# Loads issued earlier, two scale computations and one product shifted, in a fused attention and SwiGLU kernel

## The chip, the core and the metric

The kernel runs on one core of one Trainium2 chip. The metric is the device time of one execution in microseconds; the kernel before has a median of 1759.77 us over 3 runs (1759.59 to 1762.96). The core's engines are PE (matrix products), DVE, ACT and POOL (elementwise work on vectors), and SP, which here only issues DMAs. Each engine executes its own instructions in the order in which they are written; semaphores tie the engines together.

## The reference

Two branches on the same input x (2048 rows of 576), mixed row by row by a gate.

```python
x = A_x                                              # (1, 2048, 576)
g = sigmoid((x * gate_w).sum(-1, keepdims=True))
a = A_ref(x, wq, wk, wv, wo, beta)                   # attention with memory
b = (silu(x @ w_gate) * (x @ w_up)) @ w_down         # 576 -> 4608 -> 576
return g * a + (1 - g) * b

def A_ref(...):              # 32 heads of 18, 4 segments of 512 rows
    for s in range(4):
        logits = qs @ ks.T * 18 ** -0.5 + causal_mask
        a_dot = softmax(logits) @ vs
        a_mem = (phi(qs) @ M) / (phi(qs) @ z + 1e-6)     # phi(t) = t + 1 if t > 0 else exp(t)
        o = sigmoid(beta) * a_mem + (1 - sigmoid(beta)) * a_dot
        M, z = M + phi(ks).T @ vs, z + phi(ks).sum(rows)
    return o @ wo
```

## The kernel before

All operands are float32. The kernel keeps the accuracy by splitting an operand into a high and a low part and summing three products (high·high, high·low, low·high). The parts of the FFN's first two products are 16 bit, and so that they stay in range, each weight and x is first multiplied by a power of two, which is found from the data. Those factors live in columns of the tile `sc`: `sx` for x, `sw[i]` for the weights of four f-tiles (i = 0 to 8), and `iw[i]` is the inverse of both.

**Segments, 0 to 232 us.** For each of the four segments of 512 rows come nine chains of products for q and k (`qk`, 14 matmuls at L172 each, ended by conversions on ACT, DVE and POOL), and eight steps for v (`v_step`, n = 0 to 7, also L172, into banks 5, 6, 7 in turn, evacuated by ACT L434, L435 and DVE L436, and in the last four by DVE L440 too). `mem_step` (L506 and DVE L509 to L513) follows each v step in segments 1 to 3. Meanwhile the factors are found: `gauge` takes sums of squares or peaks of x and of the first weights (DVE L135, ACT L132), `total` adds them up, and `power` adds over the partitions with one small matmul (L141, into bank 7) and takes a power of two on DVE (L142 to L146). In segment 1 `power(sx)` comes after v step 1 and `power(sw[0])` after v step 5. In segment 2 the last 64 rows of x's 576 are fetched for the first half (`rest_load`), summed on POOL (`rest_sum`) and converted on ACT L197 and DVE L198 (`rest_split`); the table `RSTEP` says in which chain of the nine each of them is issued (a negative number is a sum).

**Half 0 of the FFN, 232 to about 906 us; half 1, about 911 to 1600 us.** The rows are worked in two halves (`HALF`), each with a loop over 36 f-tiles of 128 columns of w_gate and w_up. One f-tile is seven products of blocks, in place of eight, of sums and differences of blocks of x and of the weights (`seven`: six matmuls at L1303 of the kept part, one at L1306 of the 64 last rows), and after each comes a `tick`. A tick calls `beat`, and a beat does three things: it runs the functions that were deferred to it (`defer(k, fn)` is k beats on), issues groups of the down product (L1088, added up by DVE L1097), and moves the attention on by one or more steps when its credit is full. There are 8 beats to an f-tile. PE's order, and that of every other engine, is the order in which these calls are made.

For half 0, `w_make` splits the weights of the next f-tile (POOL L318, ACT L322, DVE L326) and stores them (L330) for half 1, where `w_fetch` reads them back (L821). The down weights of f are loaded with `d_load` (L266, into one of two slots `draw`), split by `d_split` (ACT L1069, DVE L1070) and stored (L1071); half 1 loads them back with L1076. `glance` loads weights of later f-tiles in full (eight loads, slots `looks`) and sums their squares on ACT (L132). Each load is issued by SP, whose queue holds also the stores, which wait there for their data.

With a position in the triple of f-tiles q = f % 3 and a tick k, the calls in half 0 are

```python
if (q, k) in ((0, 3), (1, 3), (2, 1)):
    draw[f] = d_load(f)
if (q, k) in ((1, 1), (1, 7), (2, 5)):
    g = f - 1 if k == 1 else f
    ds[half, g] = d_split(g, draw.pop(g))
```

In the last two f-tiles of half 0, `rest_second` loads the last rows of x for the second half (L1259) and converts them (ACT L1271). The first matmuls of half 1 follow the evictions L1377, L1380 (ACT) and L1384 (DVE) of the seven products.

**Attention.** `att_gen` is a generator; its step tau is one of five banks of a unit u of two heads (64 units). Most units are direct: `t_bank` computes the logits keys by queries (L957), ACT takes the exponential (L961), POOL masks (L969), DVE and POOL split it into p1 and p2 (L1055, L1057), and four steps after the unit's last bank `pv_step` multiplies all five with v (L985, L987). Ahead of that `s_bank` has found the largest logit of each row (L846 on PE, L864 on DVE). In half 1 every even unit is turned instead: its logits are exponentiated queries by keys, split (ACT L898, DVE L902, POOL L903) and transposed by DMAs (L907), and `pv_turned` multiplies (L919, L920). `v_fetch` (L254) loads v for four units at a time into one of two tiles, every 20 steps.

**End, about 1676 to 1757 us.** Attention and memory are added, multiplied with wo (L172 again), mixed with the FFN by the gate and stored (L1465).

Of the kernel before, what the change touches and what calls it, by code (L numbers as in the profile page):

```python
# [28 lines left out]
FT = 36  # L29
# [38 lines left out]
def gated_mix(ctx, tc, xT, xrest, wf, wfr, wfh, wd, wv, wo, beta, cmask, ident, bmask, out):  # L68
# [274 lines left out]
    with ExitStack() as st:  # L343
# [270 lines left out]
            rest_16(XR[j], rr[((0, 0), (0, 0), (1, 1), (0, 1), (1, 0), (1, 1), (0, 1))[j]])  # L614

        XR = [None] * 7
        RSTEP = {4: (0, 3, -1), 5: (5, -4, 1), 6: (-2, 4), 7: (2, -6), 8: (6,)}
        rb, rs = {}, {}

        def b_load(i):  # L620
# [67 lines left out]
        for s in range(NSEG):  # L688
            upd = upd_gen(s - 1) if s else None
            casts = []  # L690
            for n, (m, u) in enumerate(chains):
                mid = []
                if s == 0:
                    for z in loads.get(n, []):
                        z()
                    if n + 3 < 9:
                        mid.append(lambda n=n: q_split(*chains[n + 3]))
                    if n in halves:
                        mid.append(lambda n=n: v_split(*halves[n]))
                if s == 1 and n < 3:  # L700
                    cast = masks(*((0, 3), (3, NT), (0, 0))[n])
                    casts.append(cast)
                if s == 1 and 3 <= n < 6:
                    mid.append(casts[n - 3])
                if (s, n) == (1, 7):
                    mid.append(betas)
                mid += scan_step(17 * s + n)
                if (s, n) == (1, 7):
                    mid.append(lambda: total(sx, 0, 20))
                if s == 2:  # L710
                    if n == 4:
                        mid.append(lambda: total(sw[1], 29, 38))
                    if n == 6:
                        mid.append(lambda: power(sw[1], lone_tile([P, 1])))
                        mid.append(lambda: back(1))
                    if n == 2:
                        rest_load()
                    if n > 2 and blocks:
                        mid.append(lambda z=blocks.pop(0): b_step(*z))
                    for j in RSTEP.get(n, ()):  # L720
                        mid.append(lambda j=j: rest_split(j) if j >= 0 else rest_sum(-j))
                if s == 3:
                    if n < 4:
                        first_load(n)
                    for j, z in FSPLIT.get(n, []):
                        if j in (0, 3, 5):
                            mid.append(lambda j=j, z=z: first_split(j, z))
                    for j, z in FSUM.get(n, []):
                        mid.append(lambda j=j, z=z: first_sum(j, z))
                    for j, z in FSPLIT.get(n, []):  # L730
                        if j in (1, 2, 4):
                            mid.append(lambda j=j, z=z: first_split(j, z))
                if s < 3:
                    for kt in ((0, 1), (2, 3), (4,))[n - 6] if s == 0 and n > 5 else (n - 4,) if s and n > 3 else ():
                        raws["x", kt] = x_load(s + 1, kt)
                qk(s, m, u, mid)
                flush(2)
                scan_load(17 * s + n)
                if upd is not None and n > 0:
                    next(upd, None)  # L740
            if s == 3:
                qst_.close()
                rp = pool(ctx, "rp", 4, side="right")
                wop = pool(ctx, "wop", 8, side="right")
                kq = pool(ast, "kq", 1, side="right")
                for i in range(NST):
                    if i < 2:
                        qst.append(kq.tile([P, 2, L], BF, name=f"qst{i}"))
                    if i < 2:
                        kst.append(kq.tile([P, 2, L], BF, name=f"kst{i}"))  # L750
                for i in range(2):
                    mbs.append(kq.tile([P, 8], F32, name=f"mb{i}"))
                wraw_of[0] = [w_load(0, u) for u in range(2)]
                for z in range(2):
                    rhs.append(wop.tile([P, 7, P], F16, name=f"rh{z}", bufs=1))
                start = w_make(0)
            for n in range(8):
                hf, i = divmod(n, 4)
                flush()
                v_step(s, hf, i)  # L760
                scan_load(17 * s + 9 + n)
                if s == 1:
                    if n == 1:
                        power(sx, lone_tile([P, 1]))
                    if n == 2:
                        total(sw[0], 20, 29)
                    if n == 5:
                        power(sw[0], lone_tile([P, 1]))
                        back(0)
                if s:  # L770
                    mem_step(s, n // 2, n % 2)
                if s < 3:
                    if n == 0:
                        xs_of[s + 1] = x_tiles(s + 1)
                    if 1 <= n < 6:
                        x_split(xs_of[s + 1], n - 1, raws["x", n - 1])
                else:
                    if n == 4:
                        wraw_of[1] = [w_load(1, u) for u in range(2)]
                    if n < 2:  # L780
                        first_split(6, n)
                    elif n < 6:
                        if n < 4:
                            nc.gpsimd.memset(rhs[n - 2][96:], 0.0)
                        if n == 3:
                            r_fetch(0)
                        if n - 2 < len(kst):
                            nc.gpsimd.memset(kst[n - 2], -1.0)
                    if n > 2:
                        for z in stack_loads(0)[2 * n - 6:2 * n - 4]:  # L790
                            nc.sync.dma_start(*z)
                    for _ in range((0, 0, 2, 3, 3, 3, 3, 3)[n]):
                        if start[0][0] < 8:
                            start.pop(0)[1]()
# [5 lines left out]
    with ExitStack() as st:  # L800
# [76 lines left out]
        turned = set()  # L877
# [128 lines left out]
        def att_gen():  # L1006
            N = 10 * NB
            for tau in range(N + TL + VL + 5):
                u, n = divmod(tau, 5)
# [18 lines left out]
                if z >= 0 and z % 10 == 9:  # L1028
                    o_step(z // 10)
                z = tau - TL - VL - 1  # L1030
                if z % 5 == 4 and 0 <= z < N and z // 5 not in turned:
                    for k in range(z - 4, z + 1):
                        pv_step(k)
# [4 lines left out]
                z = tau - TL  # L1038
# [243 lines left out]
        def glance(i, k):  # L1282
            f, u = 4 * i + k // 2, k % 2
            box = []

            def load():
                box.append(x_slot(*next(looks), F32).rearrange("p a b -> p (a b)")[:, :NT * P])
                nc.sync.dma_start(box[0].rearrange("p (k n) -> p k n", n=P), wf[f][:, u])

            return [((0, 0, 1, 2, 3, 4, 4, 5)[k], load),  # L1290
                    ((2, 2, 3, 4, 5, 6, 6, 7)[k], lambda: square(box[0], 20 + 9 * i + k))]

        looks = cycle([(6, 0), (6, 1), (5, 0), (5, 1)])
# [17 lines left out]
        for pos, (half, f) in enumerate(seq):  # L1311
# [7 lines left out]
            if nxt:  # L1319
# [4 lines left out]
                if half == 0 and f + 2 < FT:  # L1324
                    wraw_of[f + 2] = [None, None]
                    for u in range(2):
                        plan.append(((2, 5)[u], lambda u=u, f=f: wraw_of[f + 2].__setitem__(u, w_load(f + 2, u))))
            i = 1 + pos // 3
            if half == 0 and pos % 3 == 0 and 2 <= i < FT // 4:
                for k in range(8):  # L1330
                    plan += glance(i, k)
            if half == 0 and pos % 3 == 1 and 2 <= i < FT // 4:
                plan += [(1, lambda i=i: total(sw[i], 20 + 9 * i, 28 + 9 * i)),
                         (5, lambda i=i: power(sw[i], ts_tile([P, 1]))), (6, lambda i=i: back(i))]
# [5 lines left out]
            if pos == 34:  # L1340
                XR2 = [None] * 7
                third = rest_second(XR2)
                plan += [(7, fn) for o, fn in third if o < 0]
            if pos == 35:
                plan += [(o, fn) for o, fn in third if o >= 0]
            for o, fn in plan:
# [3 lines left out]
            def tick():  # L1350
                k = step[0]
                step[0] += 1
                if k == 0:
                    while stores:
                        nc.sync.dma_start(*stores.pop(0))
                if half == 0:
                    if (q, k) in ((0, 3), (1, 3), (2, 1)):
                        draw[f] = d_load(f)
                    if (q, k) in ((1, 1), (1, 7), (2, 5)):
                        g = f - 1 if k == 1 else f  # L1360
                        ds[half, g] = d_split(g, draw.pop(g))
                elif (q, k) in ((1, 0), (1, 2), (2, 1)):
                    g = f - 1 if k == 0 else f
                    ds[half, g] = d_fetch(g)
                if half and k > 1:
                    opened[0] = 1
                beat(k, half)
# [157 lines left out]
```

## Time and profile before

| | |
|---|---|
| median of 3 runs | 1759.77 us |
| the profiled execution | 1760.42 us, of it span 1758.7 us |
| mean granted PE clock | 0.997 |
| PE busy | 1717.3 us, 98% |
| DVE | 1316.9 us, 75% |
| ACT | 1024.8 us, 58% |
| POOL | 843.9 us, 48% |
| DMA | 321.89 MB, mean 183 GB/s |

"Busy" adds up the instructions of an engine. In a row of the waits stand the engine and line that waited, the tile and line that ended the wait, the sum, the number of waits and the longest. In a row of the timeline stand start, duration, engine, line, operation with its tiles and shapes, number of instructions, and in brackets how long the engine had been idle before it and who ended that. SPq is SP's queue of instructions that issue DMAs; its times are those of issuing, not of the transfer.

### The profile page before, as it was taken

The page shows a single profiled execution, that of the slowest core. Times are in us where ns is not written, and L with a number is a line of the kernel's source. Part 1 is how long each engine was busy: PE and PEld are TensorE (multiplying, and loading weights), DVE is VectorE, ACT ScalarE, POOL GpSimd, SP SyncE. Part 2 cuts the span into 40 slices and gives each one's busy share as a digit, 9 for nine tenths or more (in the row PEclk, how much of TensorE's full clock was granted, in tenths as well). Part 3 has the DMA queues.
Part 4 walks back from the last instruction along what each step waited for, and adds up shares of the span by engine and source line. Part 5 has one row for each costly group of instructions (what it writes and reads, how often), then busy time and mean ns, then how long its engine had stood idle before and what let it go on. Part 6 is the DMA issues. An engine that isn't in the chain of part 4 may idle for free.

```text
span 1758.7 us, 34840 instructions
## 1 busy us (share of the span) xinstructions
PE 1717.3 (98%) x12241; PEld 1217.9 (69%) x12241; DVE 1316.9 (75%) x3239; ACT 1024.8 (58%) x1800; POOL 843.9 (48%) x1065
## 2 busy tenths in 40 slices
PE   9999999999999999999989999999999999999999
PEld 7888856656765676567657757756756766776699
DVE  6778676778878878888876877777767777775455
ACT  7757575766676666655754565555556465454411
POOL 3335551245645554665542765555546465553121
PEclk9999999999999999999999999999999999999999
DMA  8666775776676666545544487577677569654544
GB/s 286 227 219 222 233 254 192 222 229 190 180 242 219 197 186 198 183 141 156 168 149 157 121 187 167 145 196 159 142 185 196 127 162 203 168 129 129 180 137 140
DMA packets 341667, 321.89 MB, mean 183 GB/s; under 512 B 193396, under 2 KB 258676, under 8 KB 341492
## 3 DMA queue, kind: packets, MB, share of 16 engines
q1 hardware_dynamic: 341492, 319.67, 63.4%
q8 instruction: 96, 1.57, 0.4%
q14 instruction: 79, 0.65, 0.1%
HBM read 188.51 MB, written 104.86 MB: 167 GB/s over the span
## 4 chain that ended last, share of the span: by engine, by line
PE 72%; DVE 7%; ACT 6%; DMA 5%; issue 3%; SPq 3%; POOL 3%; DVEq 0%; ACTq 0%; POOLq 0%
PE bank L1303 28%; PE bank L1088 21%; PE bank L172 8%; PE bank L1306 5%; PE bank L846 3%; PE bank L957 2%; PE bank L985 1%; DMA draw<-in_wd_dram 1%; DMA xo<-in_wf_dram 1%; POOL p L1057 1%; PE bank L987 1%; SPq L1023 1%; PE bank L919 1%; ACT L1296 1%; POOL ws L318 1%
## 5 line engine op out<-in xcount | busy, mean ns | idle before, releaser
L1088 PE MATMUL bank<-dw,hh 128*128 128x320 f32 (+1 forms) x2304 | 510.5, 314 | 8.8 <-DVE ya L1097 6.8
L1088 PEld LDWEIGHTS bank<-dw,hh 128*128 128x128 f32 x2304 | 380.6, 190 | 34.2 <-DVE ya L1097 10.4
L1088 PE MATMUL bank<-dw,hl 128*128 128x320 f32 (+1 forms) x1152 | 341.0, 296 | 0.5 <-DVE hl L125 0.5
L1057 POOL TENSOR_TENSOR p<-pe,p 128x512 f16<-128x512 f32 x220 | 274.2, 1247 | 81.6 <-DVE p L1055 61.2
L961 ACT ACTIVATE pe<-bank 128x512 f32<-128x512 f32 x220 | 130.4, 593 | 218.4 <-PE bank L957 195.9
L1097 DVE TENSOR_TENSOR ya<-bank,ya 128x320 f32<-128x320 f32 x352 | 157.6, 452 | 99.6 <-PE bank L1088 97.1
L1088 PEld LDWEIGHTS bank<-dw,hl 128*128 128x128 f32 x1152 | 218.5, 190 | 1.0 <-DVE hl L125 1.0
L1306 PE MATMUL bank<-xr,rh 128*128 128x512 f16 x504 | 191.6, 380 | 0.0
L969 POOL TENSOR_SCALAR_AFFINE_SELECT pe<-pe 128x256 f32<-128x256 f32 (+1 forms) x220 | 92.2, 419 | 205.6 <-ACT pe L961 201.6
L864 DVE CUSTOM_DVE_ANT_0 junk<-bank,cm 128x128 bf16<-128x128 f32 (+2 forms) x352 | 169.7, 482 | 15.0 <-PE bank L846 9.9
L318 POOL TENSOR_TENSOR ws<-raw 128x256 f32<-128x256 f32 x72 | 66.6, 925 | 152.9 <-DMA raw<-in_wf_dram 89.6
L846 PE MATMUL bank<-kst,qst 108*128 108x512 bf16 (+3 forms) x512 | 125.2, 300 | 2.6 <-ACT pe L961 2.1
L1188 DVE TENSOR_TENSOR hl<-row,hh 128x512 fp32r<-128x512 f32 x120 | 108.5, 904 | 15.8 <-ACT hh L1187 15.4
L1055 DVE CAST p<-pe 128x512 f16<-128x512 f32 x220 | 106.3, 484 | 0.0
L1392 DVE TENSOR_TENSOR row<-bank,row 128x512 f32<-128x512 f32 x72 | 49.7, 690 | 73.6 <-ACT bank L1391 73.3
L957 PE MATMUL bank<-qst,kst 111*128 111x512 bf16 (+3 forms) x352 | 104.2, 303 | 0.0
L1387 ACT ACTIVATE row<-bank 128x512 f32<-128x512 f32 x72 | 42.9, 596 | 96.4 <-PE bank L1306 96.4
L172 PE MATMUL bank<-xo,qhi 128*128 128x512 f32 x288 | 91.8, 399 | 0.2 <-DVE xo L125 0.2
L1306 PEld LDWEIGHTS <-rh 128*128 128x128 f16 x504 | 49.4, 98 | 59.8 <-issue 0.6
L1391 ACT ACTIVATE bank<-bank 128x512 f32<-128x512 f32 x72 | 41.9, 582 | 82.2 <-PE bank L1306 80.3
L903 POOL TENSOR_TENSOR xo<-xr,xo 128x512 f16<-128x512 f32 x60 | 70.9, 1181 | 34.2 <-DVE xo L902 25.5
L416 POOL TENSOR_TENSOR q<-qr,q 128x512 bf16<-128x512 f32 x36 | 47.2, 1311 | 78.2 <-ACT q L415 64.6
(1067 smaller groups left out, 4119.2 us busy)
## 6 DMA issues: line engine op xcount, KB each, us to landing
xo<-in_wf_dram SPq DMA_DIRECT2D x65, 320.0 KB
dc<-dw SPq DMA_DIRECT2D x36, 576.0 KB
dw<-dc SPq DMA_DIRECT2D x36, 576.0 KB
raw<-in_wf_dram SPq DMA_DIRECT2D x72, 256.0 KB
rh<-rc SPq DMA_DIRECT2D x72, 168.0 KB
draw<-in_wd_dram SPq DMA_DIRECT2D x36, 288.0 KB
xo<-in_xT_dram SPq DMA_DIRECT2D x33, 256.0 KB
vd<-vps SPq DMA_DIRECT2D x8, 912.0 KB
```

The costliest lines, as they stand in the source:

```text
L172: nc.tensor.matmul(t, st[n], mv[n], start=(n == 0), stop=(n == 13))
L846: nc.tensor.matmul(t[:, c:c + w], qs[:KR, pr, P * i:P * i + P], ks[:KR, pr, 0:w], start=True, stop=True)
L864: nc.vector.tensor_tensor_reduce(junk.bitcast(BF)[:, :w], t[:, c:c + w], cm[:, L - w:L], 1.0, -3.0e38, OP.add, OP.max, m[:, k:k + 1])
L957: nc.tensor.matmul(t[:, c:c + w], ks[:KR + 3, pr, P * j:P * j + P], qs[:KR + 3, pr, P * j:L], start=True, stop=True)
L961: nc.scalar.activation(pe, t, AF.Exp, scale=SCALE)
L1055: nc.vector.tensor_copy(p1, pe)
L1057: nc.gpsimd.tensor_sub(p2, pe, p1)
L1088: nc.tensor.matmul(t, p, q[:, cs], start=(f == CH * c and n == 0), stop=(f == CH * c + CH - 1 and n == 2))
L1097: nc.vector.tensor_add(ya[:, i, cs], t, ya[:, i, cs])
L1188: defer(k + 1, lambda: nc.vector.tensor_sub(lo, src, f32(hi)))
L1303: nc.tensor.matmul(t, w[:, p, z], x[z][:, q], start=first and n == 0, stop=False, skip_group_check=True)
L1306: nc.tensor.matmul(t, rem[:, RPOS[j]], XR[j], start=False, stop=True, skip_group_check=True)
```

## The change

1. `RSTEP` and `rest_load`: in segment 2 the load of the last rows moves from chain 2 to chain 0, and the seven conversions and four sums, before in chains 4 to 8, are spread over chains 2 to 8.
2. `power(sx)` in segment 1 comes after v step 3 (before: 1), `power(sw[0])` and `back(0)` after v step 6 (before: 5).
3. In `att_gen` the products with v of a direct unit whose preceding unit is turned are issued one step later.
4. The first four of `glance`'s eight loads are issued one or two beats sooner; the first two of them in the f-tile before.
5. The first two loads of `rest_second` are issued three beats sooner.
6. The loads of the down weights are issued at (0, 1), (1, 0) and, for the next f-tile, (1, 5), where before they were at (0, 3), (1, 3) and (2, 1).

Arithmetic, tiles and the number of instructions stay the same.

```diff
-        RSTEP = {4: (0, 3, -1), 5: (5, -4, 1), 6: (-2, 4), 7: (2, -6), 8: (6,)}
+        RSTEP = {2: (0, 3), 3: (5, -1), 4: (1,), 5: (-4,), 6: (4, -2), 7: (2, -6), 8: (6,)}
...
-                    if n == 2:
+                    if n == 0:
                         rest_load()
...
                 if s == 1:
-                    if n == 1:
+                    if n == 3:
                         power(sx, lone_tile([P, 1]))
                     if n == 2:
                         total(sw[0], 20, 29)
-                    if n == 5:
+                    if n == 6:
                         power(sw[0], lone_tile([P, 1]))
                         back(0)
...
                 z = tau - TL - VL - 1
+                z -= z // 5 > 0 and (z - 1) // 5 - 1 in turned
                 if z % 5 == 4 and 0 <= z < N and z // 5 not in turned:
                     for k in range(z - 4, z + 1):
                         pv_step(k)
...
-            return [((0, 0, 1, 2, 3, 4, 4, 5)[k], load),
+            return [((-2, -1, 0, 1, 3, 4, 4, 5)[k], load),
                     ((2, 2, 3, 4, 5, 6, 6, 7)[k], lambda: square(box[0], 20 + 9 * i + k))]
...
+            if half == 0 and pos % 3 == 2 and 1 <= i < FT // 4 - 1:
+                looked = [z for k in range(8) for z in glance(i + 1, k)]
+                plan += [(7 + o, fn) for o, fn in looked if o < 0]
             if half == 0 and pos % 3 == 0 and 2 <= i < FT // 4:
-                for k in range(8):
-                    plan += glance(i, k)
+                plan += [z for z in looked if z[0] >= 0]
...
-                plan += [(7, fn) for o, fn in third if o < 0]
+                plan += [(4, fn) for o, fn in third if o < 0]
...
-                    if (q, k) in ((0, 3), (1, 3), (2, 1)):
-                        draw[f] = d_load(f)
+                    if (q, k) in ((0, 1), (1, 0), (1, 5)):
+                        g = f + (q == 1 and k == 5)
+                        draw[g] = d_load(g)
```

## The prediction

> **What bounds the kernel now.** I read the page's first part, then the waits of PE, the waits of ACT, and last the timeline around each place that the change touches.
>
> ```profile
> PE 1717.3 (98%) x12241; PEld 1217.9 (69%) x12241; DVE 1316.9 (75%) x3239; ACT 1024.8 (58%) x1800; POOL 843.9 (48%) x1065
> ```
>
> PE runs 1717.3 of the span's 1758.7 us. It executes in the order written, so the work behind an idle stretch moves up by as much as the stretch shrinks, unless another wait ends later. No edit here takes a matmul away; only PE's 41.4 us of not being busy, and stretches in which it runs slowly, can change. The waits of PE (engine, line, releaser: us in total, times, longest) say who causes them:
>
> ```profile
> PE bank L1088 <- DVE ya L1097: 6.8, 13, 1.4
> PE bank L1303 <- ACT bank L1377: 6.2, 6, 2.0
> PE bank L987 <- POOL p L1057: 5.1, 4, 2.0
> PE bank L172 <- DVE r L436: 3.9, 2, 2.6
> PE bank L1303 <- DVE bank L1384: 2.3, 2, 2.0
> ...
> PE bank L141 <- DVE dn L509: 1.2, 1, 1.2
> ...
> PE bank L172 <- DVE sc L142: 0.6, 1, 0.6
> ```
>
> The first row is not touched. The other six are each the end of a chain that one of the edits moves.
>
> **Down weights (half 0).** In six steps PE waits for ACT's eviction L1377 at the head of an f-tile. Two of those rows and the largest, with what stands ahead of it (start, duration, engine, [idle before and releaser]):
>
> ```profile
> 236.47 1.46 PE L1303 MATMUL bank<-xo,wo__2589 128*128 128x512 f16 x6 [0.80 <-ACT bank L1377]
> 248.22 1.46 PE L1303 MATMUL bank<-xo,wo__2841 128*128 128x512 f16 x6 [0.53 <-ACT bank L1377]
> ...
> 599.10 0.55 SPq L297 DMA_DIRECT2D rc<-rt  x1
> ...
> 601.34 0.46 SPq L266 DMA_DIRECT2D draw<-in_wd_dram  x1
> ...
> 607.95 0.77 ACT L1069 ACTIVATE dw<-draw,sc 128x576 fp32r<-128x576 f32 x1 [2.35 <-DMA draw<-in_wd_dram]
> 608.63 0.58 ACT L1377 ACTIVATE bank<-bank 128x512 f32<-128x512 f32 x1
> 609.26 1.46 PE L1303 MATMUL bank<-xo,wo__7517 128*128 128x512 f16 x6 [2.00 <-ACT bank L1377]
> ```
>
> ACT takes L1069 ahead of the eviction and stands 2.35 us for the weights that SP began to load at 601.34; PE pays 2.00 of it. The edit issues that load two beats earlier, ahead of the store at 599.10, so 2.2 us or more sooner; the two slots of draw are free by then, since the last reader of each (L1070) runs two beats ahead of the new place. In the waits of ACT these stalls are
>
> ```profile
> ACT xo L132 <- DMA xo<-in_wf_dram: 20.3, 15, 2.1
> ...
> ACT dw L1069 <- DMA draw<-in_wd_dram: 6.7, 5, 2.3
> ```
>
> five in all. The first two PE waits of the group (0.80 and 0.53) stand at the start of half 0, where no L1069 is late, so 6.2 − 1.33 = 4.9 us of PE's wait hang on it. What is late next is 601.34 − 599.10 = 2.24 us of advance against 2.35 us of wait, about 0.1 left in the worst place. I take −4.6; bounds −4.9 and −2.5 (half of the advance lost because the raw weight loads now queue behind).
>
> **Rests of x, second half (the step from half 0 to half 1).**
>
> ```profile
> 900.74 0.32 SPq L330 DMA_DIRECT2D wc<-wo__11429  x1
> ...
> 903.59 2.14 SPq L1259 DMA_DIRECT2D raw<-in_xr_dram  x2
> ...
> 907.90 0.72 ACT L1271 ACTIVATE xr<-raw,sc 128x512 f16<-128x512 f32 x1 [1.61 <-DMA raw<-in_xr_dram]
> ...
> 909.47 0.58 ACT L1380 ACTIVATE row<-bank 128x512 f32<-128x512 f32 x1
> ...
> 910.37 0.70 DVE L1384 TENSOR_TENSOR bank<-bank,row 128x512 f32<-128x512 f32 x1
> ...
> 911.12 2.56 PE L1303 MATMUL bank<-xo,wo__11503 128*128 128x512 f16 x6 [1.99 <-DVE bank L1384]
> ...
> 913.90 1.87 PE L1303 MATMUL bank<-xo,wo__11503 128*128 128x512 f16 x6
> ```
>
> The chain is load, L1271, L1380, L1384, PE. Three beats earlier in the list is not three beats on the chip: SP executes in order, and in the changed program the two loads stand right behind the store at 900.74, which waits for its data. So they gain 903.59 − 901.06 = 2.5 us, more than the 1.61 that ACT waits. ACT's earlier work ends at 907.90 − 1.61 = 906.29, so L1384 can end up to 1.6 earlier and PE's 1.99 shrinks to about 0.4: −1.6. Behind the wait the six matmuls take 2.56 and 1.87 where the rows above show 1.46, a stretch at half the clock: 2.56 + 1.87 − 2 × 1.46 = 1.5 us, which goes if the wait goes. Sum −3.1; bounds −3.5 and −1.0 (a transfer as late as before by 1 us).
>
> **The product with v one tick later (half 1).** PE waits for POOL's second half of p (L1057) at four odd units. The first and the last:
>
> ```profile
> 1025.09 0.19 PE L987 MATMUL bank<-v,p 128*128 128x38 bf16 x1 [0.28 <-POOL p L1057]
> ...
> 1296.48 0.19 PE L987 MATMUL bank<-v,p 128*128 128x38 bf16 x1 [2.05 <-POOL p L1057]
> ...
> 1296.90 2.64 PE L1303 MATMUL bank<-xo,wo__16820 128*128 128x512 f16 x6
> ...
> 1299.75 1.80 PE L1303 MATMUL bank<-xo,wo__16864 128*128 128x512 f16 x6
> ```
>
> The first has no turned unit ahead of it and isn't moved; the other three hold 5.1 − 0.28 = 4.8 us. One attention tick holds at least one group of seven matmuls, 1.46 plus 0.22 of PE work, and mostly two, against a longest wait of 2.05, so I count all of it gone. Behind the 2.05 again stands a half-clock stretch: 2.64 + 1.80 − 2.92 = 1.5. Together −6.3; bounds −6.5 and −4.
>
> The matmul moved last in every fourth unit also frees the tile that SP's fetch of v overwrites (L254, bufs 2), and that fetch keeps its tick. SP now stands there longer, and behind it in its queue are the transposes L907, the stack loads L1023, the operand loads L821, the down weights L1076 and L304:
>
> ```profile
> SPq L254 <- PE bank L846: 49.4, 7, 11.9
> ...
> 1041.70 0.57 SPq L821 DMA_DIRECT2D wo__13336<-wc  x1
> ...
> 1046.63 1.47 PE L1303 MATMUL bank<-xo,wo__13336 128*128 128x512 f16 x6 [0.62 <-DMA wo__13336<-wc]
> ...
> 1102.75 0.57 SPq L821 DMA_DIRECT2D wo__14252<-wc  x1
> ...
> 1108.85 1.46 PE L1303 MATMUL bank<-xo,wo__14252 128*128 128x512 f16 x6
> ```
>
> SP already stands 49.4 us there in seven places (the page names the last PE event, L846). One more tick is 1.7 to 3.4 us for each. A load that came too late needed 1046.63 − 1041.70 = 4.9 us; the tightest that I found behind a fetch, issued at 1102.75 and used at 1108.85, has 6.1, so 1.2 to spare. Most have more. Price +0.3; bounds 0 and +3.
>
> **Powers of two (segment 1).** The waits of 1.2 (L141 <- L509) and 0.6 (L172 <- L142) lie at the old places: −1.8. But the little product L141 writes bank 7, and the v products take banks 5, 6, 7 in turn; after steps 3 and 6 the bank just filled is bank 7, so each power must wait for that product's eviction. How long that takes is seen at an untouched step:
>
> ```profile
> 101.78 0.83 PE L506 MATMUL bank<-Mm,ph 128*128 128x152 f32 x6
> ...
> 102.80 0.46 DVE L436 TENSOR_TENSOR r<-bank,vps 128x288 f32<-128x288 f32 x1 [0.29 <-ACT vps L435]
> ```
>
> The product's end is the start of L506, 101.78; its last reader ends at 103.26, so 1.48 us. Step 6 has one reader more (L440), some 0.2. Two waits of 1.48 and 1.7 come, 1.8 goes: +1.4. Bounds −1.8 (nothing new waits) and +3.
>
> **Rest of x, first half (segment 2).** The load goes two chains up, and the seven rest conversions spread over chains 2 to 8.
>
> ```profile
> 140.22 2.32 DVE L198 SCALAR_TENSOR_TENSOR xr<-xo,sc,xr 32x512 f16<-32x512 f32 x2
> ...
> 157.54 0.45 DVE L436 TENSOR_TENSOR r<-bank,vps 128x288 f32<-128x288 f32 x1
> 158.04 1.86 PE L172 MATMUL bank<-vw,xo 128*128 128x288 f32 x12 [2.58 <-DVE r L436]
> ```
>
> DVE is busy without a pause from there to 157.54, and PE's 2.58 is that backlog. A step of two L198 is 2.32; half of it, 1.2, is what moving two conversions ahead of the backlog is worth, less 0.2 for a new wait ahead of it: −1.0. Bounds −2.6 (the whole wait) and 0.
>
> **Looks at the weights:** four of the eight loads go one or two beats sooner. The 20.3 us that ACT waits at L132 shrink, but none of PE's seven rows names L132 or something right behind it: 0; bounds −1.5 and +0.5.
>
> **Sum.** −4.6 − 3.1 − 6.3 + 0.3 + 1.4 − 1.0 = −13.3. The profiled execution took 1760.42 (span 1758.7 and 1.7 around it), 0.65 over the median 1759.77. So span 1745.4, profiled 1747.1, and median 1746.5.
>
> [...] Half clock follows the waits of 1.99 and 2.05, but not those of 2.00 (609.26) and 2.58 (158.04, where 12 matmuls take 1.86). So length alone doesn't decide it. [...]
>
> **The rivals.**
> 1. The slow stretches are not caused by the waits in front of them and stay, wherever they fall: 3.0 of the sum goes, 1749.5. Two of four such waits are followed by none, which speaks for it; that they begin at the wait, against. [...] Chance 0.12.
> 2. The loads take their time from other loads: each one that goes ahead holds back a raw weight or an operand. Then the down-weight gain halves (2.3), the rest's goes (3.1), the powers cost 3 instead of 1.4 and the fetches 3 instead of 0.3: −13.3 + 9.7 = −3.6, 1756.2. For it: ACT and POOL wait on loads in many places. Against: the bytes are the same, only their order changes. Chance 0.12.
> 3. Slower. The fetch of v, held a tick longer, passes its hold on to PE: eight times the hold of up to 3.4 less 1.2 to spare, 2.2, and half a clock behind each, 1.5, are 29.6: −13.6 + 29.6 = +16, 1776. It decides from 1.7 us for each fetch on. Against it are the 6.1 us at the tightest place and fetches that already stand 7 us on average with hardly a PE wait by a load. Chance 0.06.
> 4. The moved loads don't start sooner, because each still stands behind a store that waits in SP's queue: d_load and rests bring nothing, −13.3 + 7.7 = −5.6, 1754.2. The new order speaks against it at 599.10 and 900.74. Chance 0.05.
>
> **How the numbers follow.** The forecast, 1746.5, has 0.65. A measurement of this kernel tells 0.2%, 3.5 us, from no change, so faster is below 1756.3: the forecast, rivals 1 and 4, and a third of rival 2, 0.65 + 0.12 + 0.05 + 0.04 = 0.86, of which I leave 0.04 to bounds that add up badly: 0.82. Same takes most of rival 2 and some of that: 0.10; slower 0.08. The range: all low bounds together would be −4.9 − 3.5 − 6.5 − 1.8 − 2.6 − 1.5 = −20.8; they won't all come, so 1740.5. Upward to rivals 1 and 4 and the edge of 2: 1756.
>
> **What would show it.** Right: ACT's waits at L1069 (6.7) near 0; no wait of L987 on L1057 but the first; PE's wait at 911 under 0.6 and 1.46 behind it; two waits of about 1.5 at L141 on bank 7; the wait at 158 about 1 us shorter. Wrong: new PE waits on loads of wo_ in half 1 behind L254, or half-clock stretches at other places. I am wrong altogether if PE's waits shrink by 10 and the span doesn't follow.

## The result, and the profile after

The kernel after takes 1750.11 us (median of 4 runs, 1749.31 to 1750.78) against 1760.08 for the kernel before in the same measurement. The ratio is 0.994, 95% interval 0.9923 to 0.9957, so 10 us were won, inside the range and 3.6 us short of the forecast. The span of its profile is 1748.7 us against 1758.7.

The page and the waits of PE for the kernel after (from L1031 on, line numbers are one to four higher than before: L1303 is now L1304, L1377 is L1381, L1384 is L1388, L1069 is L1070, L1088 is L1089, L1057 is L1058):

```profile
PE 1714.6 (98%) x12241; PEld 1217.6 (70%) x12241; DVE 1326.4 (76%) x3239; ACT 1024.4 (59%) x1800; POOL 841.7 (48%) x1065
```

```profile
PE bank L1089 <- DVE ya L1098: 7.0, 13, 1.4
PE bank L172 <- DVE r L436: 2.2, 2, 1.1
...
PE bank L846 <- DMA kst<-stw: 2.0, 1, 2.0
PE bank L141 <- DVE r L436: 1.9, 1, 1.9
...
PE bank L141 <- DVE gl L440: 1.5, 1, 1.5
PE bank L1304 <- ACT bank L1381: 1.3, 2, 0.8
...
PE bank L1304 <- DVE bank L1388: 0.8, 2, 0.5
...
PE bank L1304 <- DMA wo__17650<-wc: 0.6, 1, 0.6
...
PE bank L987 <- POOL p L1058: 0.3, 1, 0.3
```

Four rows of before have shrunk as forecast: L1304 behind ACT from 6.2 to 1.3, L987 behind POOL from 5.1 to 0.3, L172 behind L436 from 3.9 to 2.2, and L1304 behind DVE from 2.3 to 0.8. The two rows of the powers at their old places are gone. Both waits of the powers on bank 7 are new, and they were expected. A wait of 2.0 us for a stack load kst is new and was not. One more is the prediction's own sign of being wrong, a new wait on a load of wo_ in half 1: it came once, with 0.6 us (wo__17650), while the 0.6 us of wo__13336 went. The same places in the timeline of the kernel after:

```profile
100.13 0.38 PE L141 MATMUL bank<-sc 128*128 128x1 f32 x2 [1.91 <-DVE r L436]
100.38 0.91 PE L506 MATMUL bank<-Mm,ph 128*128 128x114 f32 x6
101.08 2.70 PE L172 MATMUL bank<-vw,xo 128*128 128x290 f32 x12
...
111.51 0.35 PE L141 MATMUL bank<-sc 128*128 128x1 f32 x2 [1.52 <-DVE gl L440]
...
160.47 1.86 PE L172 MATMUL bank<-vw,xo 128*128 128x288 f32 x12 [1.11 <-DVE r L436]
...
238.67 1.46 PE L1304 MATMUL bank<-xo,wo__2589 128*128 128x512 f16 x6 [0.81 <-ACT bank L1381]
...
596.13 0.47 SPq L266 DMA_DIRECT2D draw<-in_wd_dram  x1
596.71 0.57 SPq L297 DMA_DIRECT2D rc<-rt  x1
...
603.06 0.76 ACT L1070 ACTIVATE dw<-draw,sc 128x576 fp32r<-128x576 f32 x1
603.73 0.58 ACT L1381 ACTIVATE bank<-bank 128x512 f32<-128x512 f32 x1
...
604.65 1.46 PE L1304 MATMUL bank<-xo,wo__7517 128*128 128x512 f16 x6
...
905.27 1.46 PE L1304 MATMUL bank<-xo,wo__11509 128*128 128x512 f16 x6 [0.47 <-DVE bank L1388]
...
1280.46 0.39 SPq L1023 DMA_DIRECT2D kst<-stw  x1
...
1286.34 0.38 PE L846 MATMUL bank<-kst,qst 108*128 108x512 bf16 x1 [2.03 <-DMA kst<-stw]
```

What each stage cost or gave is read from the starts of the same matmuls in both profiles. The group that ran at 236.47 before runs at 238.67: up to the start of half 0 the change has lost 2.2 us. The first group of half 1 that waits stood at 911.12 and stands at 905.27 (it is the same group; its tile is numbered wo__11503 before and wo__11509 after): half 0 and the handover gave 2.2 + 5.85 = 8.05. The span is 10.0 shorter, so half 1 and the end gave 4.15. By the two pages PE's time of not being busy fell from 1758.7 − 1717.3 = 41.4 us to 1748.7 − 1714.6 = 34.1, which is 7.3 of the 10.0; the other 2.7 are less busy time, for the same number of matmuls.

### The profile page after: what moved, and what is told of

Read it like the earlier page. It is cut to its first block, busy times and chain, and to the rows that moved or that the text cites. A ratio compares the mean times of both kernels' runs of the same rounds, so it can differ in the third digit from the quotient of the medians.

```text
span 1748.7 us, 34878 instructions
## 1 busy us (share of the span) xinstructions
PE 1714.6 (98%) x12241; PEld 1217.6 (70%) x12241; DVE 1326.4 (76%) x3239; ACT 1024.4 (59%) x1800; POOL 841.7 (48%) x1065
## 4 chain that ended last, share of the span: by engine, by line
PE 79%; DVE 7%; ACT 5%; DMA 3%; issue 3%; SPq 2%; POOL 1%; DVEq 0%; ACTq 0%; POOLq 0%
PE bank L1304 33%; PE bank L1089 23%; PE bank L172 7%; PE bank L1307 5%; PE bank L846 4%; PE bank L957 2%; PE bank L985 2%; PE bank L987 1%; DMA stw<-q 1%; PE bank L919 1%; ACT L1297 1%; DVE xo L1242 1%; PE bank L460 1%; ACT L1398 1%; DMA wo__21835<-wc 0%
## 5 line engine op out<-in xcount | busy, mean ns | idle before, releaser
L1089 PE MATMUL bank<-dw,hh 128*128 128x320 f32 (+1 forms) x2304 | 510.0, 314 | 9.2 <-DVE ya L1098 7.0
L1089 PEld LDWEIGHTS bank<-dw,hh 128*128 128x128 f32 x2304 | 380.3, 190 | 35.0 <-DVE ya L1098 11.1
L1089 PE MATMUL bank<-dw,hl 128*128 128x320 f32 (+1 forms) x1152 | 341.0, 296 | 0.6 <-DVE hl L125 0.5
L1058 POOL TENSOR_TENSOR p<-pe,p 128x512 f16<-128x512 f32 x220 | 273.5, 1243 | 88.1 <-DVE p L1056 60.6
L1089 PEld LDWEIGHTS bank<-dw,hl 128*128 128x128 f32 x1152 | 218.4, 190 | 1.1 <-DVE hl L125 1.1
L846 PE MATMUL bank<-kst,qst 108*128 108x512 bf16 (+3 forms) x512 | 125.2, 300 | 5.4 <-ACT pe L961 2.1
L1396 DVE TENSOR_TENSOR row<-bank,row 128x512 f32<-128x512 f32 x72 | 49.7, 691 | 70.7 <-ACT bank L1395 70.3
L172 PE MATMUL bank<-xo,qhi 128*128 128x512 f32 x288 | 91.9, 399 | 0.6 <-DVE xo L125 0.5
```

The source lines that it names most:

```text
L172: nc.tensor.matmul(t, st[n], mv[n], start=(n == 0), stop=(n == 13))
L846: nc.tensor.matmul(t[:, c:c + w], qs[:KR, pr, P * i:P * i + P], ks[:KR, pr, 0:w], start=True, stop=True)
L1058: nc.gpsimd.tensor_sub(p2, pe, p1)
L1089: nc.tensor.matmul(t, p, q[:, cs], start=(f == CH * c and n == 0), stop=(f == CH * c + CH - 1 and n == 2))
```

## The experiments

Each kernel was compared with the kernel before in the same measurement; a ratio r means a gain of (1 − r) × 1760 us.

**Down weights alone (d_alone).** The kernel before, with

```diff
-                    if (q, k) in ((0, 3), (1, 3), (2, 1)):
-                        draw[f] = d_load(f)
+                    if (q, k) in ((0, 1), (1, 0), (1, 5)):
+                        g = f + (q == 1 and k == 5)
+                        draw[g] = d_load(g)
```

> The kernel before with the down-weight loads alone moved. Theory (from the two traces): PE's five waits behind L1069 go, 4.9 us by the rows, and each stop of PE costs some 0.16 us more than its row shows, so -5.7 us; the waits of the down products on DVE at 336, 514 and 573 us stay. Rival 1: the rows say all, -4.6 as predicted. Rival 2: those DVE waits hang on these loads too, then about -6.8.

Ratio 0.9968 (0.9957 to 0.9979), −5.6 us. The row of ACT's waits at L1069 is gone. The size fits the theory. Of the small waits on L1097 that were to stay, the one at 336 us (0.34 us before) is gone, as it is in kernels without this edit; the one near 514 us (0.33 before) stands at 0.49; at 573 us the profile of before has only 0.07. The rows speak against rival 2, which ties these waits to the loads; the interval alone holds the theory's −5.7 and both rivals.

**Looks alone (g_alone).** The kernel before, with

```diff
-            return [((0, 0, 1, 2, 3, 4, 4, 5)[k], load),
+            return [((-2, -1, 0, 1, 3, 4, 4, 5)[k], load),
...
```

> The kernel before with the looks at the weights alone moved. Theory: ACT reaches L300 sooner, so the store of the rests and DVE L282 behind it are sooner, and PE's waits on DVE L1097 at 336, 514 and 573 us go: -1.3 us. Rival, the prediction: no PE wait follows L132, 0 us.

Ratio 0.9994 (0.9982 to 1.0006), no difference that can be told. ACT's 20.3 us at L132 are gone from the waits, and its wait at L1069 is 6.7 us as before. The time can't tell the theory's −1.3 us from the prediction's 0. PE's waits on DVE at 336 and 514 us vanish in this profile, as the theory has it, but the one at 336 us is also gone in the profiles of d_alone and pow_alone, and both are gone in that of rs_alone (below), which all keep the looks where they were. So the looks are not shown to be their cause.

**The product with v alone (pv_alone).** The kernel before, with

```diff
                 z = tau - TL - VL - 1
+                z -= z // 5 > 0 and (z - 1) // 5 - 1 in turned
```

> The kernel before with the product with v alone moved. Theory: the waits on L1057 at 1115, 1176 and 1296 us go, but the fetch of v holds SP about 3 us longer, and near 1294 us PE waits about 2 us for a stack load kst instead: -3 us in all, with SP's wait at L254 near 70 us. Rival, the prediction: no load comes late, -6 us.

Ratio 0.9983 (0.997 to 0.9996), −3.0 us. PE's wait for kst and SP's longer wait are both there:

```profile
1285.73 0.40 SPq L1023 DMA_DIRECT2D kst<-stw  x1
...
1291.86 0.38 PE L846 MATMUL bank<-kst,qst 108*128 108x512 bf16 x1 [1.29 <-DMA kst<-stw]
```

```profile
SPq L254 <- PE bank L846: 70.1, 8, 14.5
```

That the one causes the other is not shown by this run.

**Powers alone (pow_alone).** The kernel before, with

```diff
-                    if n == 1:
+                    if n == 3:
                         power(sx, lone_tile([P, 1]))
...
-                    if n == 5:
+                    if n == 6:
                         power(sw[0], lone_tile([P, 1]))
```

> The kernel before with the two powers alone moved. Theory: the two waits for bank 7 are 1.9 and 1.5 us in place of 1.2 and 0.6, and the longer one is followed by some 4 us at half the clock, +1.7: +3.4 us in all. Rival, the prediction: the waits alone, +1.4 us. If the slow stretch is a matter of chance and falls out here, the waits are the same and the sum is +1.7.

Ratio 1.0022 (1.001 to 1.0034), +3.9 us: this part alone makes the kernel slower. Its timeline:

```profile
100.44 0.38 PE L141 MATMUL bank<-sc 128*128 128x1 f32 x2 [1.91 <-DVE r L436]
100.68 0.99 PE L506 MATMUL bank<-Mm,ph 128*128 128x114 f32 x6
101.42 3.25 PE L172 MATMUL bank<-vw,xo 128*128 128x290 f32 x12
...
105.53 1.86 PE L172 MATMUL bank<-vw,xo 128*128 128x290 f32 x12
...
111.77 0.35 PE L141 MATMUL bank<-sc 128*128 128x1 f32 x2 [1.52 <-DVE gl L440]
```

Both waits are as in the kernel after, and the 12 matmuls behind the first take 3.25 us where 12 of the same shape take 1.86 four microseconds later.

**Powers on another bank (p_bank1).** The kernel after, with

```diff
-                        power(sx, lone_tile([P, 1]))
+                        power(sx, x_tile([P, 1]))
...
-                        power(sw[0], lone_tile([P, 1]))
+                        power(sw[0], x_tile([P, 1]))
```

> The kernel after, with the two powers in their new places but on bank 1, which no v product uses, in place of bank 7. Theory: both waits at L141 (1.9 and 1.5 us) and the slow stretch behind the first are the price of bank 7 and go: 5 us under the kernel after, ratio to before about 0.9915. Rival: the powers wait for their own sums on DVE, which only come this late; then the waits move to L142 or stay, and the time stays at 0.994.

Ratio 0.9909 (0.9894 to 0.9924), median 1745.87 us. The timeline has neither wait nor slow stretch:

```profile
97.99 0.28 PE L141 MATMUL bank<-sc 128*128 128x1 f32 x2
98.13 0.91 PE L506 MATMUL bank<-Mm,ph 128*128 128x114 f32 x6
98.83 1.86 PE L172 MATMUL bank<-vw,xo 128*128 128x290 f32 x12
...
106.00 0.28 PE L141 MATMUL bank<-sc 128*128 128x1 f32 x2
```

So the bank was the cause, not the sums. This version is faster than the kernel before, and by the two ratios 5.5 us under the kernel after, which was measured at another time; v_plus1 and v_plus5 below, which keep the powers on bank 7, were measured beside it and are 4.3 and 3.4 us slower.

**Powers back in their old places (p_old)**, the rest as after (the edit of the powers alone, reversed).

> The kernel after with the two powers back in their old places. Theory: the waits of 1.2 and 0.6 us come back and those of 1.9 and 1.5 go, with the slow stretch behind the first: 1.7 to 3.3 us under the kernel after, and 1.8 to 2.1 above the version with the powers on bank 1, so a ratio to before of about 0.992. Rival: the shift of the powers does something for the stages behind it; then no gain on the kernel after (0.994).

Ratio 0.9923 (0.9911 to 0.9936), median 1747.0 us, as the theory had it; the rival's 0.994 lies just outside. So with bank 7 the old places are the better ones. The old places with bank 1 were not run, so what the move itself is worth stays open.

**The fetch of v one step, and five steps, later (v_plus1, v_plus5).** The kernel after, with TL + VL + 2 and, in the second, TL + VL + 6 in

```diff
-                z = tau - TL - VL - 1
+                z = tau - TL - VL - 2
                 if z % 20 == 0 and 0 <= z < N and z // 20 + 1 < 4 * NSEG:
                     v_fetch(z // 20 + 1)
```

> The kernel after, with the fetch of v issued one attention step later, so that it has its old place behind the product that frees its tile. Theory: SP's wait at L254 falls from 71 to about 50 us, and PE's wait of 2.0 us for the stack load kst at 1286 us goes or falls under 0.5: about 2 us under the kernel after. Rival: that load was late before as well and was only covered by the wait on L1057; then PE's wait there stays near 2 us whatever SP does.

> The kernel after, with the fetch of v issued five attention steps later, by when its tile has long been free. Theory: SP hardly waits at L254 (under 10 us), every load behind it in the queue goes sooner, and PE's waits for kst (2.0) and wo_ (0.6 at 1341 us) go: 2 to 2.6 us under the kernel after. Rival: v itself then comes late for the turned products, and PE waits at L919 for it: the same time or more.

Ratios 0.9934 (0.992 to 0.9948) and 0.9929 (0.9917 to 0.9942): neither can be told from the kernel after. SP's wait at L254 for L846 falls from 70.7 to 14.9 us, more than expected, and with five steps its row is gone. With one step:

```profile
1275.74 0.52 SPq L1023 DMA_DIRECT2D kst<-stw  x1
...
1282.36 0.38 PE L846 MATMUL bank<-kst,qst 108*128 108x512 bf16 x1 [0.53 <-DMA kst<-stw]
...
1292.41 0.38 PE L957 MATMUL bank<-qst,kst 111*128 111x512 bf16 x1 [1.11 <-DVE acc L930]
```

With five steps:

```profile
1275.53 0.40 SPq L1023 DMA_DIRECT2D kst<-stw  x1
...
1283.69 0.38 PE L846 MATMUL bank<-kst,qst 108*128 108x512 bf16 x1 [1.71 <-DMA kst<-stw]
```

The theory falls in its size, and half of its mechanism holds. Call lead the time from the load's issue to where PE would have used it without the wait. In the kernel after it is 1286.34 − 2.03 − 1280.46 = 3.9 us, with one step 6.1, and the wait for kst falls from 2.03 to 0.53. So SP's hold at L254 does make this load late. But no time comes of it, since 10 us later PE stops 1.11 us for a bank. The same pair stands between p_bank1 and bank1_v1 (below): 1.42 falls to 0.31, and the same 1.11 comes. What sets that 1.11 was not tested. The rival of the first edit, a wait near 2 us whatever SP does, doesn't hold there. In the kernel before this load was issued at 1288.85 and first used behind the wait on L1057, at 1296.68; without that wait its lead would have been 5.8 us.

With five steps the lead is 6.5 us, and PE still waits 1.71, because the load took 8.2 us from issue to use, against 5.2 to 6.6 in the other profiles that wait for it. The windows (us, busy time of PE, PEld, DVE, ACT, POOL with the number of instructions, clock, DMA share, GB/s), first of the kernel after, then with five steps, show DMA shares of 1.14 and 1.06, and of 0.99:

```profile
1275.00:1280.00 5.00, 5.00 (x26) 2.40 (x25) 2.60 (x6) 4.97 (x10) 3.15 (x5) 1.00 1.14 237
1280.00:1286.30 6.30, 4.31 (x22) 2.00 (x21) 6.30 (x20) 4.12 (x9) 3.70 (x5) 1.00 1.06 302
```

```profile
1275.50:1283.70 8.20, 6.49 (x34) 3.04 (x33) 6.55 (x20) 6.27 (x13) 5.21 (x8) 1.00 0.99 278
```

With one step the share is 0.98 from issue to use as well, and there the load took 6.6 us. So the share alone doesn't explain the 8.2; its cause stays open.

**Both: powers on bank 1 and the fetch one step later (bank1_v1).** The two edits above together.

> The kernel after with the powers on bank 1 and the fetch of v one step later. Theory: the fetch of v alone brought nothing at its place (2.0 us of PE's wait for kst went, 1.5 came back as a wait for a bank that DVE L930 frees), so this is no faster than the powers on bank 1 alone: ratio to before 0.990 to 0.991. Rival: half a microsecond to 2 us more, 0.989 to 0.990.

Ratio 0.9915 (0.9902 to 0.9928), median 1745.55: no faster than the powers on bank 1 alone.

**Rests of the first half alone (rs_alone).** The kernel before, with

```diff
-        RSTEP = {4: (0, 3, -1), 5: (5, -4, 1), 6: (-2, 4), 7: (2, -6), 8: (6,)}
+        RSTEP = {2: (0, 3), 3: (5, -1), 4: (1,), 5: (-4,), 6: (4, -2), 7: (2, -6), 8: (6,)}
...
-                    if n == 2:
+                    if n == 0:
                         rest_load()
```

> The kernel before with the rests of x for the first half alone spread over chains 2 to 8. Theory: PE's wait at 158 us falls from 2.6 to 1.1, and with it goes the half-clock stretch of 1.3 to 1.5 that stands behind that wait in most executions, though not in the profile of before: -3 us. Rival, the prediction: -1.0.

Ratio 0.9978 (0.9968 to 0.9988), −3.9 us, nearer to the theory than to the prediction. The wait at 158 us, here and in d_alone, which leaves these rests where they were:

```profile
156.42 1.85 PE L172 MATMUL bank<-vw,xo 128*128 128x288 f32 x12 [1.11 <-DVE r L436]
```

```profile
158.59 3.25 PE L172 MATMUL bank<-vw,xo 128*128 128x288 f32 x12 [2.60 <-DVE r L436]
```

The profile of before shows 2.58 and 1.86 there: the same wait, without the slow stretch.

**Rests of the second half alone (r_alone).** The kernel before, with

```diff
-                plan += [(7, fn) for o, fn in third if o < 0]
+                plan += [(4, fn) for o, fn in third if o < 0]
```

> The kernel before with the first loads of the second half's rests alone moved. The prediction: -3.1 us. Rival: in the runs that leave these loads where they were, PE's wait at about 911 us was 2.0, 1.8, 1.7, 1.4, 2.8 and 2.7 us, with a half-clock stretch behind two of the six; so the profile of before was one of the dearer draws, and the edit is worth the wait's fall to some 0.5 plus a third of 1.5: -1.5 to -2.2 us.

Ratio 0.9995 (0.9986 to 1.0003), −0.9 us (−2.5 to +0.5): the prediction's −3.1 lies outside the interval, the rival's −1.5 to −2.2 lies inside, and 0 does too.

## Why the prediction was right, and where its steps were off

In us, the prediction's terms beside what each part alone measured:

| part | predicted | measured alone |
|---|---|---|
| down weights | −4.6 | −5.6 (−7.6 to −3.7) |
| rests, second half | −3.1 | −0.9 (−2.5 to +0.5) |
| product with v | −6.3 + 0.3 | −3.0 (−5.3 to −0.7) |
| powers | +1.4 | +3.9 (+1.8 to +6.0) |
| rests, first half | −1.0 | −3.9 (−5.6 to −2.1) |
| looks | 0 | −1.1 (−3.2 to +1.1) |
| sum | −13.3 | −10.6; the whole change −10.0 to −10.6 |

The base held: PE is busy for 98% of both spans, and the span fell by what PE's waits and slow stretches fell. The parts add up to the whole as far as intervals of about 2 us on each can tell. Where an interval excludes nought, the sign is the predicted one; for four parts the predicted size lies outside the interval. That the total came within 3.6 us is in part luck: by the middle values three parts gave 7.7 us less than predicted and three gave 5.0 more.

*Powers.* The bank and the waits were right: 1.48 and 1.7 were expected, 1.91 and 1.52 came, and p_bank1 shows that bank 7 is the cause. The term that failed is the clock behind the wait, which the prediction had counted at two other places and not at its own new wait: 3.25 or 2.70 us for the 12 matmuls in place of 1.86. Two of the four profiles with this wait show the stretch.

*Rests of the first half.* The same step failed the other way round. The wait falls from 2.58 to 1.11, 1.5 where 1.0 was expected; and the prediction took the absence of a slow stretch behind 2.58 as a property of the place. Of the six profiles that have this wait five show the stretch, and that of before is the sixth; the last section shows where the wait of before fell.

*Rests of the second half.* In the six profiles that leave these loads alone the wait is 1.39 to 2.81, on average 2.06, so the 1.99 of before was no odd draw; but the stretch stands behind only two of the six. With the edit the wait is 0.46 or 0.47 in five of seven profiles, and 1.44 in p_bank1 and 1.62 in bank1_v1, for a reason that was not tested. The step that failed is the 1.5 us of the slow stretch, which the prediction counted as sure.

*Product with v.* The three waits went, as predicted. The step that failed is the price of +0.3 for SP's longer hold at L254. The hold grew by 70.7 − 49.4 = 21.3 us over eight fetches, 2.7 each and within the 1.7 to 3.4 that the prediction gave; but the prediction looked for the tightest load among those of wo_, with 1.2 us to spare, and the load that came late is one of kst (L1023), a line that it had named and for which it shows no lead. PE waits 1.29 us for it in pv_alone and 2.03 in the kernel after; the prediction's upper bound of +3 covers that. That the hold causes the wait is shown by v_plus1 and bank1_v1; that a kernel without the hold is faster is not. The slow stretch counted behind the 2.05 is a smaller fault: it stands in five of six profiles, not in all. What is left of the 3 us lies within the interval.

*Down weights.* Right. The measured −5.6 is 1 us more; a stop that costs more than its row (below) would give 0.8 of it, but the interval doesn't exclude the −4.6.

The rival that the slow stretches are not caused by the waits falls: apart from the last 2 us of an execution, every one of the 22 half-clock stretches in the 13 profiles begins in a wait or at most 1.7 us behind its end (0.04 to 1.64 us behind it in those of before and after), and where the wait went (at 100 us in p_bank1) or fell to 1.1 (at 158 us in rs_alone) there is none. A wait of 1.91 us at L141 had the stretch behind it twice, in the kernel after and in pow_alone. The same wait at the same place is followed by the stretch in some profiles and not in others, and in the profiles of before and after the stretches start a whole number of steps of 3.413 us apart (last section).

## What to carry to other kernels

Before a wait is taken away, ask what else moves with the work behind it. Here the tile was freed one step later, SP's queue stood 70.7 us behind that in place of 49.4, and a load further down the queue became the new wait, of 2.03 us; when the load got its lead back, a bank became the next, with 1.11. A small operation that is moved to a better time still needs a free bank there: the move alone cost 3.9 us, and placing the operation on bank 1, which the v steps around it do not use, won 3.4 us or more back. The waits near 2 us here had up to 1.7 us of lost clock behind them in some profiles and none in others. One profile shows one draw of that, so price it by its chance over several.

## What the runs showed of the hardware

**Half the clock behind some of the short waits.** In the record of the granted clock of the kernels before and after, each of the five stretches ahead of the last 2 us has the clock at 0.50 and lasts 3.41 us, so it costs up to 1.7 us. In the kernel before they start at 911.31, 921.55 and 1297.02 us (the prediction saw the first and the last), 3 and 110 steps of 3.413 us apart; in the kernel after they start at 101.77 and 914.14, 238 steps apart. Counted from the start of each execution, the steps of the two profiles are shifted by 0.58 us. These are windows of one step in the kernel before, for PE alone (length in us, busy time of PE with the number of its instructions, clock, DMA share, GB/s):

```profile
907.90:911.31 3.41, 1.42 (x7) 1.00 0.89 340
911.31:914.73 3.42, 3.42 (x9) 0.50 0.41 111
153.55:156.97 3.42, 1.92 (x16) 1.00 0.00 0
156.97:160.38 3.41, 2.33 (x18) 1.00 0.68 197
160.38:163.80 3.42, 3.42 (x28) 1.00 0.78 258
```

The wait of 1.99 us at 911 us lies wholly in one window, and the next window runs at half the clock. The longer wait of 2.58 us at 158 us is split, 1.50 us in one window and 1.08 in the next, and the clock stays at 1.00. These two profiles have six waits of 1.9 to 2.8 us. The two of the kernel before with 1.99 and 2.05 us in one window, at 911 and 1296 us, are followed by half the clock. Of the four with at most 1.89 in any window (1.50 of the 2.58 at 158 us and 1.73 of the 2.00 at 609 us before, 1.77 of the 1.91 at 100 us and 1.89 of the 2.03 at 1286 us after) one is, that at 100 us. This is read from the record; no run shifted a wait against these windows.

Over the 13 profiles PE has 28 waits of 1.9 to 2.8 us, of which 15 are followed by half the clock. By place it is 5 of 6 at the wait of 2.58 at 158 us, 5 of 6 at that of 2.0 to 2.3 on L1057, 2 of 4 at L141, 2 of 3 at 911 us, 1 of 7 at the heads of f-tiles behind ACT, and 0 of 2 for kst. In the kernels before and after none of the 14 waits of 1.10 to 1.72 us that stood alone has one. Near 915 us a wait of 1.3 to 1.6 and one of 0.2 to 0.5 follow each other within 3 us, and seven of the 13 profiles show a stretch there. So the idle time in one window doesn't decide alone: 1.49 us had the stretch behind it there in the kernel before, the 1.73 us of the wait at 609 us had not.

This is also the kernel's own spread. In the 62 executions of the kernel before that were measured beside the experiments, the mean granted clock is 0.996 in eleven, which took 1761.4 to 1766.6 us, and 0.999 or 1.000 in seven, which took 1755.4 to 1758.3. One stretch, 1.7 of 1759 us, is worth 0.001 of that mean. The same wait without and with, r_alone first and before second (its wait of 2.05 stands in the prediction):

```profile
1297.36 0.19 PE L987 MATMUL bank<-v,p 128*128 128x38 bf16 x1 [2.05 <-POOL p L1057]
...
1297.77 1.46 PE L1303 MATMUL bank<-xo,wo__16820 128*128 128x512 f16 x6
```

```profile
1296.90 2.64 PE L1303 MATMUL bank<-xo,wo__16820 128*128 128x512 f16 x6
```

**A stop cost 0.16 us more than its row.** Here matmuls of 0.38 us start 0.21 to 0.22 apart, so in a row of them each covers 0.16 of the next; a stop uncovers it. In the kernel before:

```profile
605.37 0.38 PE L1306 MATMUL bank<-xr,rh 128*128 128x512 f16 x1
605.58 1.46 PE L1303 MATMUL bank<-xo,wo__7517 128*128 128x512 f16 x6
606.88 0.38 PE L1306 MATMUL bank<-xr,rh 128*128 128x512 f16 x1
```

The next group starts at 609.26, not at 606.88 + 0.21 = 607.09: 2.17 late, behind a wait whose row says 2.00. Five such waits would make 0.8 us of the 1 us by which the down weights gave more than predicted. The 0.38 is the profile's duration of one matmul; the starts alone give the 2.17.
